# State@W in 64x32 array tiles, and x transposed by DMA, in a PE-bound attention and GLU kernel

## The chip, the core, the metric

The kernel runs on one core of a Trainium2 chip. The metric is device microseconds of one execution. PE is the matmul engine, DVE the vector engine, ACT the scalar engine, POOL is GpSimd, and SP is the engine that issues the DMAs. "Granted clock" is the share of full speed that PE was allowed. PSUM is where matmuls leave their results; ACT or DVE copies these out, which the text calls evacuation. A weight load (PEld) brings PE the stationary operand of a matmul. A profile is one execution; its span is 1.7 to 2.0 us shorter than that execution's time. Times between starts of instructions in a profile repeat to a few hundredths of a microsecond; whole executions of a kernel vary by 2 to 3 us.

## The reference

```python
# attention: B, H, S, Ns, D = 8, 8, 512, 32, 64
scores = x @ state^T / sqrt(D);  a = softmax(scores, -1);   xread = a @ state
scores2 = state @ x^T / sqrt(D); a2 = softmax(scores2, -1); sread = a2 @ x
y = concat([xread, sread], axis=2)            # per batch 512 + 32 rows of 512
# GLU: d_model 512, d_ff 1536
out = (sigmoid(y @ w_gate) * (y @ w_val)) @ w_out
```

Both kernels use that (a @ state) @ W = a @ (state @ W), so the 512 xread rows of a batch never exist; the product state@W (SW) does, once for each batch.

## The kernel before

A batch is worked on in twelve steps f. In step f PE computes a part of the output of batch b-1, then one block of gate and value (`gv`) of batch b, and between them pieces for batch b+1: one PSUM tile of SW, and at certain steps a piece of attention.

```python
p_gv  = tile_pool(bufs=3, PSUM); p_out = tile_pool(bufs=1, PSUM)
p_sw  = tile_pool(bufs=2, PSUM); p_at  = tile_pool(bufs=2, PSUM)

def at_xT(b, i):                 # x transposed on PE, copied out by DVE
    for jj in range(2):
        for c in range(4):
            nc.tensor.transpose(ps[:, jj, c], xbs[b][:, c, ...], ident)
    nc.vector.tensor_copy(xTs[b][:, 2*i:2*i+2], ps)

def sw_tile(b, t):               # one PSUM tile: heads of two j; half of each operand is zero
    for jj in range(2):
        lo = j * 128 - 64 * jj
        nc.tensor.matmul(ps, flat[:, lo:lo + 128], W[:, j, q*512:(q+1)*512], ...)
    nc.scalar.activation(SWs[b][:, g, w, q*512:(q+1)*512], ps, AF.Copy)

def gv(b, f):                    # two PSUM tiles, two matmuls each
    ...
    nc.scalar.activation(th, pss[0], AF.Tanh, scale=0.5)
    nc.vector.scalar_tensor_tensor(glus[b][:, f], th, 1.0, pss[1], ALU.add, ALU.mult)

    # one step, b > 0
    out_mm(b - 1, f); gv(b, f); sw_tile(nb, f)
    # f: 0, 1 at_xT   2, 3 at_S (scores, exp)   4, 5 at_norm   6 at_aT   8 at_sr
```

`at_norm` (DVE) makes `ab`, the normalised attention; `at_aT` transposes it on PE; `at_sr` is sread. Batch 0 runs while the weights are loaded and cast. "Batch 8" is no batch of its own: it is the GLU of the 256 sread rows of all batches.

The softmax here doesn't subtract the row's maximum and nothing guards it: scores larger than these inputs give would overflow.

## Time and profile before

| | before |
|---|---|
| time, median of 3 runs | 279.37 us (279.27 to 280.76) |
| span of the profiled run (another execution, of 281.71 us) | 279.9 us |
| first gv matmul | 20.62 us |
| batch 1 begins (first output matmul) | 54.02 us |
| one of batches 1 to 6 | 28.94 us (the sixth 28.74) |
| batch 7 begins | 227.44 us |

A batch's beginning is read from the order of time: the start of its first group of output matmuls. The difference between two beginnings is what a batch costs, waits included, and it is free of the overlap that makes a sum of durations misleading. The lines themselves stand in the prediction.

### The profile page before, as it was taken

The numbers are of one execution on the slowest core, as the hardware profiler recorded it, in microseconds if no ns is written. First come the engines' busy times: TensorE is split into PE (matmuls) and PEld (weight loads), VectorE is DVE, ScalarE is ACT, GpSimd is POOL, SyncE is SP. The second block draws the span as 40 slices with busy tenths as digits, with TensorE's granted clock in tenths as the row PEclk, the third lists the DMA queues.
The fourth block names the chain that finished last, engine by engine and source line by source line (L and its number), as shares of the span: only waits on it lengthen the run. The fifth ranks groups of instructions, "written<-read, shape, count | busy, mean of one in ns | idle before, by whom it ended". The sixth has DMA issues, their size and how long they took to land.

```text
span 279.9 us, 4309 instructions
## 1 busy us (share of the span) xinstructions
PE 260.1 (93%) x1670; PEld 136.5 (49%) x1670; DVE 132.0 (47%) x212; ACT 153.0 (55%) x264; POOL 40.4 (14%) x86
## 2 busy tenths in 40 slices
PE   6588857999999999999999999999999999999993
PEld 6564322554545454544554455445454544456651
DVE  4376273646544554446543744385338523332210
ACT  3368684656555755575557555655575554433220
POOL 1360089004000500050003100220010000000000
PEclk9979796999999999999999999999999999999999
DMA  7999738010016100611160015100101110110213
GB/s 239 368 378 386 250 115 290 3 41 37 37 32 174 42 27 31 187 40 37 39 190 37 37 41 176 51 37 37 40 37 39 40 39 37 75 40 37 77 39 75
DMA packets 18245, 27.55 MB, mean 98 GB/s; under 512 B 944, under 2 KB 9136, under 8 KB 18224
## 3 DMA queue, kind: packets, MB, share of 16 engines
q1 hardware_dynamic: 18224, 27.27, 28.8%
q8 instruction: 13, 0.21, 0.3%
q14 instruction: 8, 0.07, 0.1%
HBM read 18.35 MB, written 8.91 MB: 97 GB/s over the span
## 4 chain that ended last, share of the span: by engine, by line
PE 81%; DVE 10%; ACT 4%; issue 1%; DMA 1%; ACTq 0%
PE outp L209 29%; PE gvp L192 26%; PE swp L177 13%; PE gvp L195 4%; PE xTp L107 3%; DVE glu L200 2%; DVE rs L131 2%; DVE ab L134 2%; PE aTp L141 1%; DMA sf<-in_state_dram 1%; PE srp L157 1%; PE srp L152 1%; PE Sp L117 1%; DVE ri L133 1%; ACT th L199 1%
## 5 line engine op out<-in xcount | busy, mean ns | idle before, releaser
L200 DVE SCALAR_TENSOR_TENSOR glu<-th,gvp 128x512 bf16<-128x512 f32 (+1 forms) x108 | 70.9, 656 | 123.4 <-ACT th L199 108.0
L209 PE MATMUL outp<-wo,glu 128*128 128x512 bf16 x408 | 104.1, 379 | 0.7 <-ACT res L213 0.7
L192 PE MATMUL gvp<-aT,SW 128*128 128x512 bf16 x384 | 99.9, 382 | 0.1
L199 ACT ACTIVATE th<-gvp 128x512 f32<-128x512 f32 (+1 forms) x108 | 61.8, 572 | 63.4 <-PE gvp L192 53.0
L179 ACT ACTIVATE SW<-swp 128x512 bf16<-128x512 f32 x96 | 57.0, 597 | 29.1 <-PE swp L177 29.1
L192 PEld LDWEIGHTS <-SW 128*128 128x128 bf16 x384 | 37.6, 99 | 46.0 <-issue 1.6
L209 PEld LDWEIGHTS <-glu 128*128 128x128 bf16 x408 | 37.9, 98 | 37.9 <-issue 1.0
L177 PE MATMUL swp<-wg,sTz 128*128 128x512 bf16 x96 | 29.5, 396 | 7.1 <-DVE wg L92 7.1
L124 POOL CAST Eb<-E 128x256 bf16<-128x256 f32 x32 | 12.4, 416 | 160.4 <-ACT E L119 160.4
L177 PEld LDWEIGHTS <-sTz 128*128 128x128 bf16 x192 | 19.1, 101 | 31.4 <-DVE wg L92 7.7
L213 ACT ACTIVATE res<-outp 128x512 f32<-128x512 f32 x34 | 20.3, 597 | 21.0 <-PE outp L209 21.0
L177 PE MATMUL swp<-wv,sTz 128*128 128x512 bf16 x96 | 29.6, 398 | 0.3 <-ACT SW L179 0.3
L89 POOL CAST xb<-xf 128x512 bf16<-128x512 f32 x28 | 16.5, 628 | 0.0
L108 DVE COPY xT<-xTp 128x1024 bf16<-128x1024 bf16 x16 | 11.1, 691 | 4.1 <-PE xTp L107 4.1
L134 DVE TENSOR_TENSOR ab<-E,ri 128x512 bf16<-128x512 f32 x16 | 12.6, 788 | 0.6
L107 PE MATMUL xTp<-ident,xb 128*128 128x128 bf16 x128 | 10.4, 225 | 2.6 <-ACT xb L267 2.5
L107 PEld LDWEIGHTS <-xb 128*128 128x128 bf16 x128 | 8.8, 101 | 6.3 <-ACT xb L267 3.0
L131 DVE TENSOR_REDUCE rs<-E 128x16 f32<-128x512 f32 x16 | 10.8, 676 | 1.2 <-ACT E L119 1.2
L119 ACT ACTIVATE E<-Sp 128x512 f32<-128x512 f32 x16 | 9.4, 592 | 1.8 <-PE Sp L117 1.8
L160 DVE RECIPROCAL r<-srp 128x128 f32<-128x128 f32 x8 | 7.7, 957 | 3.1 <-PE srp L157 3.1
L97 POOL CAST wo<-wof 128x512 bf16<-128x512 f32 x12 | 8.7, 775 | 0.0
L227 PE MATMUL warm<-ident 128*128 128x128 bf16 x62 | 6.9, 301 | 1.4 <-POOL ident masks.py:199 1.4
(39 smaller groups left out, 111.1 us busy)
## 6 DMA issues: line engine op xcount, KB each, us to landing
out_dram<-res SPq DMA_DIRECT2D x32, 256.0 KB, 2.2
xf<-in_x_dram SPq DMA_DIRECT2D x7, 1024.0 KB, 6.4
wf<-in_moe_w_gate_dram SPq DMA_DIRECT2D x3, 1024.0 KB, 11.7
wf<-in_moe_w_val_dram SPq DMA_DIRECT2D x3, 1024.0 KB, 10.7
wof<-in_moe_w_out_dram SPq DMA_DIRECT2D x3, 1024.0 KB, 8.2
xf<-in_x_dram SPq DMA_DIRECT2D x2, 512.0 KB, 5.7
sf<-in_state_dram SPq DMA_DIRECT2D x1, 512.0 KB, 4.0
out_dram<-res SPq DMA_DIRECT2D x8, 64.0 KB, 1.7
```

The source lines that it names most:

```text
L89: eng.tensor_copy(xb.rearrange("p c h d -> p h c d")[:, 2 * i:2 * i + 2], xf[:, 2 * i:2 * i + 2])
L107: nc.tensor.transpose(ps[:, jj, c], xbs[b][:, c, 2 * j:2 * j + 2].rearrange("p h d -> p (h d)"), ident)
L124: nc.gpsimd.tensor_copy(Ebs[b][:, c], E1s[b][:, c])
L131: nc.vector.tensor_reduce(rs, E, AX.X, ALU.add)
L134: nc.vector.tensor_tensor(abs_[b][:, 2 * i:2 * i + 2].rearrange("p c (h n) -> p (c h) n", n=Ns), E, ri.unsqueeze(2).to_broadcast((128, 16, ...
L177: nc.tensor.matmul(ps, flat[:, lo:lo + 128], W[:, j, q * 512:(q + 1) * 512], start=(jj == 0), stop=(jj == 1))
L179: nc.scalar.activation(SWs[b][:, g, w, q * 512:(q + 1) * 512], ps, AF.Copy)
L192: nc.tensor.matmul(ps, SWs[b][:, g, w, fs], aTs[b][:, g], start=(g == 0), stop=(g == 1))
L199: nc.scalar.activation(th, pss[0], AF.Tanh, scale=0.5)
L200: nc.vector.scalar_tensor_tensor(glus[b][:, f], th, 1.0, pss[1], ALU.add, ALU.mult)
L209: nc.tensor.matmul(ops[b, c], glus[b][:, f, c * 128:(c + 1) * 128], wo[:, f], start=(f == 0), stop=(f == NF - 1))
L213: nc.scalar.activation(res, ops[b, c], AF.Copy, scale=0.5)
```

## The change

The intent: give PE less to do. The state operand of state@W was half zeros. The new kernel lets each 64x32 block (one head's 64 rows by 32 state columns) be a matmul of its own in its own part of the array: two row halves e times four column groups j, eight at a time. The eight go to two PSUM tiles; with gate and value a "visit" makes four, so the state@W pool takes four PSUM banks and the others give some up. x of batches 1 to 7 is transposed by DMA. The loads and casts of W come in column chunks.

```diff
-    p_gv  = ... bufs=3      p_sw = ... bufs=2      p_at = ... bufs=2
+    p_gv  = ... bufs=2      p_sw = ... bufs=4      p_at = ... bufs=1
-    stg = ... bufs=5
+    stg = ... bufs=6
+    def at_xT_dma(b):
+        for c in range(4):
+            nc.sync.dma_start_transpose(xT[:, :, c], xbs[b][:, c]...)
-    def sw_tile(b, t):  ...
+    def sw_visit(b, lo, n):
+        for w in range(2):
+            pss = [p_sw.tile((128, 512), FP)[:, :n] for e in range(2)]
+            for j in range(4):
+                for e in range(2):
+                    rows = slice(e * 64, (e + 1) * 64)
+                    nc.tensor.matmul(pss[e][j * Ns:(j + 1) * Ns], sTz[rows, b, j, e],
+                                     (wg, wv)[w][rows, j, lo:lo + n], start=True, stop=True)
+            for e in range(2):
+                sw_left.append((SWs[b][:, e, w, lo:lo + n], pss[e]))
     # one step, b > 0
-                sw_tile(nb, f)
+                if f % 4 == 0:
+                    sw_visit(nb, f * 128, 512)
+                sw_evac(act)                 # one of the four tiles a step
+                if f == 0:
+                    at_xT_dma(nb)
+                    if nb + 1 < B:
+                        load_x(nb + 1)
# cut: heads split by parity e in E1, Eb, ab; batch 0's schedule rewritten (visits at
# f = 1, 3, 3, 7, 7, 10, evacuated by ACT and DVE at once; casts of W at f = 3 and 7)
```

More of the change, by code (lines that the diff above doesn't have):

```diff
@@ L39 @@
     ctx.enter_context(tc.manual_schedule())
+    PS = bass.MemoryType.PSUM
     wp = ctx.enter_context(tc.tile_pool(name="wp", bufs=1))
-    stg = ctx.enter_context(tc.tile_pool(name="stg", bufs=5))
+    stg = ctx.enter_context(tc.tile_pool(name="stg", bufs=6))
     xp = ctx.enter_context(tc.tile_pool(name="xp", bufs=2))
@@ L45 @@
     fp = ctx.enter_context(tc.tile_pool(name="fp", bufs=3))
-    p_gv = ctx.enter_context(tc.tile_pool(name="p_gv", bufs=3, space=bass.MemoryType.PSUM))
-    p_out = ctx.enter_context(tc.tile_pool(name="p_out", bufs=1, space=bass.MemoryType.PSUM))
-    p_sw = ctx.enter_context(tc.tile_pool(name="p_sw", bufs=2, space=bass.MemoryType.PSUM))
-    p_at = ctx.enter_context(tc.tile_pool(name="p_at", bufs=2, space=bass.MemoryType.PSUM))
+    p_gv = ctx.enter_context(tc.tile_pool(name="p_gv", bufs=2, space=PS))
+    p_out = ctx.enter_context(tc.tile_pool(name="p_out", bufs=1, space=PS))
+    p_sw = ctx.enter_context(tc.tile_pool(name="p_sw", bufs=4, space=PS))
+    p_at = ctx.enter_context(tc.tile_pool(name="p_at", bufs=1, space=PS))
     ident = wp.tile((128, 128), BF, name="ident")
     ones = wp.tile((128, 2, 128), BF, name="ones")
-    sTz = wp.tile((128, B, 4, 128), BF, name="sTz")
+    sTz = wp.tile((128, B, 4, 2, Ns), BF, name="sTz")
     wg = wp.tile((128, 4, dff), BF, name="wg")
@@ L60, with psum_at, load_x, load_w @@
     E1s, Ebs, abs_, aTs, SWs, glus = {}, {}, {}, {}, {}, {}
-    def load_x(b):
+    vec, act, pool = nc.vector.tensor_copy, nc.scalar.copy, nc.gpsimd.tensor_copy
+    def psum_at(b):
+        return (p_sw, "swp") if b == 0 else (p_at, "at")
+    def load_x(b, parts=1):
         xf = stg.tile((128, H, 4, D), FP, name="xf", tag="stg")
         v = x[b].rearrange("h (p c) d -> p h c d", c=4)
-        if b == 0:
-            for i in range(2):
-                nc.sync.dma_start(xf[:, 4 * i:4 * i + 4], v[:, 4 * i:4 * i + 4])
-        else:
-            nc.sync.dma_start(xf, v)
+        n = H // parts
+        for i in range(parts):
+            nc.sync.dma_start(xf[:, n * i:n * i + n], v[:, n * i:n * i + n])
         xfs[b] = xf
-    def load_w(src, key, q):
-        wf = stg.tile((128, 4, 512), FP, name="wf", tag="stg")
-        nc.sync.dma_start(wf, src.rearrange("(k p) n -> p k n", p=128)[:, :, q * 512:(q + 1) * 512])
-        wfs[key, q] = wf
+    def load_w(src, key, lo, n):
+        wf = stg.tile((128, 4, n), FP, name="wf", tag="stg", padded_shape=(128, 4, 512))
+        nc.sync.dma_start(wf, src.rearrange("(k p) n -> p k n", p=128)[:, :, lo:lo + n])
+        wfs[key, lo] = wf
     def load_wo(q):
@@ L81, in load_wo, with cast_x, cast_w @@
         wfs["o", q] = wf
-    def cast_x(b, eng, parts):
+    def cast_x(b, cp, lo, n):
         if b not in xbs:
             xbs[b] = xp.tile((128, 4, H, D), BF, name="xb")
-        xf, xb = xfs[b], xbs[b]
-        for i in parts:
-            eng.tensor_copy(xb.rearrange("p c h d -> p h c d")[:, 2 * i:2 * i + 2], xf[:, 2 * i:2 * i + 2])
-    def cast_w(q):
-        nc.vector.tensor_copy(wg[:, :, q * 512:(q + 1) * 512], wfs["g", q])
-        nc.scalar.activation(wv[:, :, q * 512:(q + 1) * 512], wfs["v", q], AF.Copy)
+        cp(xbs[b].rearrange("p c h d -> p h c d")[:, lo:lo + n], xfs[b][:, lo:lo + n])
+    def cast_w(key, cp, lo, n, parts=1):
+        w, m = (wg if key == "g" else wv), 4 // parts
+        for i in range(parts):
+            cp(w[:, m * i:m * i + m, lo:lo + n], wfs[key, lo][:, m * i:m * i + m])
     def cast_wo(q):
@@ L97, in cast_wo, with xT_tile, at_xT_pe @@
             nc.gpsimd.tensor_copy(wo[:, 4 * q + i], wfs["o", q][:, i])
-    def at_xT(b, i):
-        if i == 0:
-            xTs[b] = ap_.tile((128, 4, 512), BF, name="xT")
-        ps = p_at.tile((128, 2, 4, 128), BF, name="xTp", tag="at")
+    def xT_tile(b):
+        if b not in xTs:
+            xTs[b] = ap_.tile((128, 4, 4, 128), BF, name="xT")
+        return xTs[b]
+    def at_xT_pe(b, i, cp):
+        pool_, tag = psum_at(b)
+        ps = pool_.tile((128, 2, 4, 128), BF, name="xTp", tag=tag)
         for jj in range(2):
@@ L107, in at_xT, with at_norm @@
                 nc.tensor.transpose(ps[:, jj, c], xbs[b][:, c, 2 * j:2 * j + 2].rearrange("p h d -> p (h d)"), ident)
-        nc.vector.tensor_copy(xTs[b][:, 2 * i:2 * i + 2], ps.rearrange("p j c t -> p j (c t)"))
+        cp(xT_tile(b)[:, 2 * i:2 * i + 2], ps)
+    def at_xT_dma(b):
+        xT = xT_tile(b)
+        for c in range(4):
+            nc.sync.dma_start_transpose(xT[:, :, c], xbs[b][:, c].rearrange("p h d -> p (h d)"))
     def at_S(b, i):
         if i == 0:
-            E1s[b] = ap_.tile((128, 4, H * Ns), FP, name="E1")
-        ps = p_at.tile((128, 2, H * Ns), FP, name="Sp", tag="at")
+            E1s[b] = ap_.tile((128, 4, 2, 4, Ns), FP, name="E1")
+        pool_, tag = psum_at(b)
+        ps = pool_.tile((128, 2, 2, 4, Ns), FP, name="Sp", tag=tag)
         for cc in range(2):
-            c = 2 * i + cc
             for j in range(4):
-                nc.tensor.matmul(ps[:, cc, j * 64:(j + 1) * 64], xTs[b][:, j, c * 128:(c + 1) * 128],
-                                 sTz[:, b, j, 0:64], start=True, stop=True)
+                nc.tensor.matmul(ps[:, cc, :, j], xTs[b][:, j, 2 * i + cc], sTz[:, b, j], start=True, stop=True)
         nc.scalar.activation(E1s[b][:, 2 * i:2 * i + 2], ps, AF.Exp, scale=scale)
     def at_Eb(b):
-        Ebs[b] = ap_.tile((128, 4, H * Ns), BF, name="Eb")
+        Ebs[b] = ap_.tile((128, 4, 2, 4, Ns), BF, name="Eb")
         for c in range(4):
             nc.gpsimd.tensor_copy(Ebs[b][:, c], E1s[b][:, c])
-    def at_norm(b, i):
+    def at_norm(b, i, eng):
         if i == 0:
-            abs_[b] = ap_.tile((128, 4, H * Ns), BF, name="ab")
-        E = E1s[b][:, 2 * i:2 * i + 2].rearrange("p c (h n) -> p (c h) n", n=Ns)
+            abs_[b] = ap_.tile((128, 4, 2, 128), BF, name="ab")
+        E = E1s[b][:, 2 * i:2 * i + 2].rearrange("p c e j n -> p (c e j) n")
         rs = ap_.tile((128, 16), FP, name="rs")
@@ L133, in at_norm @@
         nc.vector.reciprocal(ri, rs)
-        nc.vector.tensor_tensor(abs_[b][:, 2 * i:2 * i + 2].rearrange("p c (h n) -> p (c h) n", n=Ns), E,
-                                ri.unsqueeze(2).to_broadcast((128, 16, Ns)), ALU.mult)
+        eng.tensor_tensor(abs_[b][:, 2 * i:2 * i + 2].rearrange("p c e (j n) -> p (c e j) n", n=Ns), E,
+                          ri.unsqueeze(2).to_broadcast((128, 16, Ns)), ALU.mult)
     def at_aT(b):
-        ps = p_at.tile((128, 2, 4, 128), BF, name="aTp", tag="at")
-        for g in range(2):
+        pool_, tag = psum_at(b)
+        ps = pool_.tile((128, 2, 4, 128), BF, name="aTp", tag=tag)
+        for e in range(2):
             for c in range(4):
-                nc.tensor.transpose(ps[:, g, c], abs_[b][:, c, g * 128:(g + 1) * 128], ident)
+                nc.tensor.transpose(ps[:, e, c], abs_[b][:, c, e], ident)
         aTs[b] = ap_.tile((128, 2, 512), BF, name="aT")
@@ L147, in at_sr @@
         ps = p_at.tile((128, 512), FP, name="srp", tag="at")
-        sr = ps[:, 0:256].rearrange("p (j e) -> p j e", j=4)
+        sr = ps[:, 0:256].rearrange("p (j e n) -> p j e n", j=4, e=2)
         sm = ps[:, 256:384].rearrange("p (j n) -> p j n", j=4)
-        for par in range(2):
+        for e in range(2):
             for c in range(4):
-                nc.tensor.matmul(sm, ones[:, par],
-                                 Eb[:, c].rearrange("p (j e n) -> p j e n", j=4, e=2)[:, :, par],
-                                 start=(par == 0 and c == 0), stop=(par == 1 and c == 3))
+                nc.tensor.matmul(sm, ones[:, e], Eb[:, c, e], start=(e == 0 and c == 0), stop=(e == 1 and c == 3))
         for j in range(4):
@@ L157, in at_sr @@
                 nc.tensor.matmul(sr[:, j], xbs[b][:, c, 2 * j:2 * j + 2].rearrange("p h d -> p (h d)"),
-                                 Eb[:, c, j * 64:(j + 1) * 64], start=(c == 0), stop=(c == 3))
+                                 Eb[:, c, :, j], start=(c == 0), stop=(c == 3))
         r2 = ap_.tile((128, 4, Ns), FP, name="r2")
@@ L161, in at_sr, with sw_evac @@
         for e in range(2):
-            nc.vector.tensor_tensor(XS[e * 64:(e + 1) * 64, :, b * Ns:(b + 1) * Ns],
-                                    sr[e * 64:(e + 1) * 64, :, e * Ns:(e + 1) * Ns],
-                                    r2[e * 64:(e + 1) * 64], ALU.mult)
-    def sw_tile(b, t):
-        if t == 0:
-            SWs[b] = fp.tile((128, 2, 2, dff), BF, name="SW", bufs=2)
-        q, w, g = t // 4, (t // 2) % 2, t % 2
-        ps = p_sw.tile((128, 512), FP, name="swp")
-        W = wg if w == 0 else wv
-        for jj in range(2):
-            j = 2 * g + jj
-            flat = sTz[:, b].rearrange("p j e -> p (j e)")
-            lo = j * 128 - 64 * jj
-            nc.tensor.matmul(ps, flat[:, lo:lo + 128], W[:, j, q * 512:(q + 1) * 512],
-                             start=(jj == 0), stop=(jj == 1))
-        nc.scalar.activation(SWs[b][:, g, w, q * 512:(q + 1) * 512], ps, AF.Copy)
+            rows = slice(e * 64, (e + 1) * 64)
+            nc.vector.tensor_tensor(XS[rows, :, b * Ns:(b + 1) * Ns], sr[rows, :, e], r2[rows], ALU.mult)
+    sw_left = []
+    def sw_visit(b, lo, n):
+        if b not in SWs:
+            SWs[b] = fp.tile((128, 2, 2, dff), BF, name="SW", bufs=2)
+        for w in range(2):
+            pss = [p_sw.tile((128, 512), FP, name="swp", tag="swp")[:, :n] for e in range(2)]
+            for j in range(4):
+                for e in range(2):
+                    rows = slice(e * 64, (e + 1) * 64)
+                    nc.tensor.matmul(pss[e][j * Ns:(j + 1) * Ns], sTz[rows, b, j, e],
+                                     (wg, wv)[w][rows, j, lo:lo + n], start=True, stop=True)
+            for e in range(2):
+                sw_left.append((SWs[b][:, e, w, lo:lo + n], pss[e]))
+    def sw_evac(cp):
+        if sw_left:
+            cp(*sw_left.pop(0))
     def gv(b, f):
@@ L194, in gv @@
                 for j in range(4):
-                    nc.tensor.matmul(ps, (wg if w == 0 else wv)[:, j, fs], XS[:, j], start=(j == 0), stop=(j == 3))
+                    nc.tensor.matmul(ps, (wg, wv)[w][:, j, fs], XS[:, j], start=(j == 0), stop=(j == 3))
             pss.append(ps)
@@ L230 @@
     nc.sync.dma_start(sf, state.rearrange("b h (u l) d -> (b h u) l d", l=16))
-    load_x(0)
-    load_w(moe_w_gate, "g", 0)
-    load_w(moe_w_val, "v", 0)
+    load_x(0, 2)
+    load_w(moe_w_gate, "g", 0, 256)
+    load_w(moe_w_val, "v", 0, 256)
+    load_w(moe_w_gate, "g", 256, 256)
+    load_w(moe_w_val, "v", 256, 256)
     load_x(1)
@@ L236 @@
     nc.vector.memset(sTz, 0.0)
-    for par in range(2):
-        nc.gpsimd.memset(ones[:, par, par * 64:par * 64 + 64], 1.0)
-        nc.gpsimd.memset(ones[:, par, 64 - par * 64:128 - par * 64], 0.0)
+    for e in range(2):
+        nc.gpsimd.memset(ones[:, e, e * 64:e * 64 + 64], 1.0)
+        nc.gpsimd.memset(ones[:, e, 64 - e * 64:128 - e * 64], 0.0)
     pre = wp.tile((128, 1), FP, name="pre")
     nc.scalar.activation(pre, ident[:, 0:1], AF.Exp)
-    warm(30)
+    warm(36)
     sb = wp.tile((128, 16, 2, D), BF, name="sb")
     nc.vector.tensor_copy(sb[:, :, 0], sf)
-    nc.scalar.activation(sb[:, :, 1], sf, AF.Copy)
-    cast_x(0, nc.vector, (0, 1))
+    nc.scalar.copy(sb[:, :, 1], sf)
+    cast_x(0, vec, 0, 4)
+    cast_x(0, act, 4, 4)
     stp = []
@@ L255, with sT_copy @@
         stp.append(ps)
-    at_xT(0, 0)
-    for i in range(2):
+    def sT_copy(i, bs, cp):
         for e in range(2):
             rows = slice(e * 64, (e + 1) * 64)
-            dst = sTz[rows, :, :, e * Ns:(e + 1) * Ns].rearrange("p b j (u l) -> p (b j) u l", u=2)[:, :, :, 8 * i:8 * i + 8]
-            src = stp[i][rows].rearrange("p l (k e u) -> p k e u l", e=2, u=2)[:, :, e]
-            if e == 0:
-                nc.vector.tensor_copy(dst, src)
-            else:
-                nc.scalar.activation(dst, src, AF.Copy)
-    for i in (2, 3):
-        nc.scalar.activation(xbs[0].rearrange("p c h d -> p h c d")[:, 2 * i:2 * i + 2], xfs[0][:, 2 * i:2 * i + 2], AF.Copy)
+            dst = sTz[rows, bs, :, e].rearrange("p b j (u l) -> p (b j) u l", u=2)[:, :, :, 8 * i:8 * i + 8]
+            src = stp[i][rows].rearrange("p l (b j e u) -> p b j e u l", b=B, e=2, u=2)[:, bs, :, e]
+            cp(dst, src.rearrange("p b j u l -> p (b j) u l"))
+    at_xT_pe(0, 0, vec)
+    sT_copy(0, slice(0, 1), vec)
+    sT_copy(1, slice(0, 1), act)
+    cast_w("g", pool, 0, 256)
+    cast_w("v", pool, 0, 256)
     warm(8)
-    at_xT(0, 1)
-    load_w(moe_w_gate, "g", 1)
-    load_w(moe_w_val, "v", 1)
+    at_xT_pe(0, 1, vec)
+    load_w(moe_w_gate, "g", 512, 512)
+    load_w(moe_w_val, "v", 512, 512)
     warm(8)
@@ L274 @@
     at_S(0, 1)
-    for k in range(4):
-        nc.gpsimd.tensor_copy(wg[:, k, 0:512], wfs["g", 0][:, k])
-    at_norm(0, 0)
-    at_norm(0, 1)
-    nc.scalar.activation(wv[:, :, 0:512], wfs["v", 0], AF.Copy)
+    sT_copy(0, slice(1, B), act)
+    at_norm(0, 0, nc.vector)
+    at_norm(0, 1, nc.vector)
+    sT_copy(1, slice(1, B), act)
+    cast_w("g", pool, 256, 256)
+    cast_w("v", act, 256, 256)
     warm(16)
-    for t in range(2):
-        sw_tile(0, t)
+    sw_visit(0, 0, 256)
+    for cp in (act, act, act, act):
+        sw_evac(cp)
     at_aT(0)
     at_Eb(0)
-    at_sr(0)
-    cast_x(1, nc.gpsimd, range(4))
+    cast_x(1, pool, 0, 4)
+    cast_x(1, pool, 4, 4)
     for b in range(B + 1):
@@ L291 @@
             nb = b + 1 if b + 1 < B else None
-            if b == 0:
-                if f % 4 == 0:
-                    for t in range(f if f else 2, f + 4):
-                        sw_tile(0, t)
-                if f == 1:
-                    load_w(moe_w_gate, "g", 2)
-                    load_w(moe_w_val, "v", 2)
-                if f in (4, 5, 6):
-                    load_wo(f - 4)
-                if f in (8, 9, 10):
-                    cast_wo(f - 8)
             if b > 0:
@@ L305 @@
             gv(b, f)
-            if nb is not None:
-                sw_tile(nb, f)
-                if b > 0 and f == 0 and nb + 1 < B:
-                    load_x(nb + 1)
-                at = f if b > 0 else f - 2
-                if at == 0:
-                    at_xT(nb, 0)
-                elif at == 1:
-                    at_xT(nb, 1)
-                elif at == 2:
+            if b == 0:
+                if f == 1:
+                    sw_visit(0, 256, 256)
+                    for cp in (act, vec, act, vec):
+                        sw_evac(cp)
+                    load_w(moe_w_gate, "g", 1024, 512)
+                    load_w(moe_w_val, "v", 1024, 512)
+                    at_xT_dma(1)
+                elif f == 2:
+                    at_sr(0)
+                elif f == 3:
+                    sw_visit(1, 0, 512)
+                    for cp in (act, vec, act, vec):
+                        sw_evac(cp)
+                    cast_w("g", vec, 512, 512)
+                    cast_w("v", act, 512, 512)
+                    at_S(1, 0)
+                    sw_visit(0, 512, 512)
+                    for cp in (act, vec, act, vec):
+                        sw_evac(cp)
+                elif f == 4:
+                    at_S(1, 1)
+                    at_Eb(1)
+                elif f == 5:
+                    at_norm(1, 0, nc.vector)
+                elif f == 6:
+                    at_norm(1, 1, nc.vector)
+                elif f == 7:
+                    sw_visit(1, 512, 512)
+                    for cp in (act, vec, act, vec):
+                        sw_evac(cp)
+                    cast_w("g", vec, 1024, 512)
+                    cast_w("v", act, 1024, 512)
+                    at_aT(1)
+                    sw_visit(0, 1024, 512)
+                    for cp in (act, vec, act, vec):
+                        sw_evac(cp)
+                elif f == 9:
+                    at_sr(1)
+                elif f == 10:
+                    sw_visit(1, 1024, 512)
+                if f in (3, 5, 7):
+                    load_wo((f - 3) // 2)
+                if f == 8:
+                    load_x(2)
+                if f in (9, 10, 11):
+                    cast_wo(f - 9)
+                if f in (10, 11):
+                    sw_evac(act)
+                    sw_evac(vec)
+            elif nb is not None:
+                if f % 4 == 0:
+                    sw_visit(nb, f * 128, 512)
+                sw_evac(act)
+                if f == 0:
+                    at_xT_dma(nb)
+                    if nb + 1 < B:
+                        load_x(nb + 1)
+                elif f == 2:
@@ L316 @@
                     at_S(nb, 0)
-                elif at == 3:
+                elif f == 3:
                     at_S(nb, 1)
-                elif at == 4:
-                    at_norm(nb, 0)
+                elif f == 4:
+                    at_norm(nb, 0, nc.vector)
                     at_Eb(nb)
-                elif at == 5:
-                    at_norm(nb, 1)
-                elif at == 6:
+                elif f == 5:
+                    at_norm(nb, 1, nc.vector)
+                elif f == 6:
@@ L325 @@
                     at_aT(nb)
-                elif at == 8:
+                elif f == 8:
                     at_sr(nb)
-                if b == 0 and f == 9:
-                    load_x(2)
-                if nb + 1 < B and f == 11:
-                    cast_x(nb + 1, nc.gpsimd, range(4))
-            if b == 0 and f in (3, 7):
-                cast_w(f // 4 + 1)
+            if nb is not None and nb + 1 < B and f == 11:
+                cast_x(nb + 1, pool, 0, 4)
+                cast_x(nb + 1, pool, 4, 4)
```

## The prediction

> **What bounds the kernel now.** I read the page's busy table and slices first, then the costliest groups, then the order of time inside one batch, then the waits.
>
> ```profile
> PE 260.1 (93%) x1670; PEld 136.5 (49%) x1670; DVE 132.0 (47%) x212; ACT 153.0 (55%) x264; POOL 40.4 (14%) x86
> PE   6588857999999999999999999999999999999993
> PEclk9979796999999999999999999999999999999999
> L209 PE MATMUL outp<-wo,glu 128*128 128x512 bf16 x408 | 104.1, 379 | 0.7 <-ACT res L213 0.7
> L192 PE MATMUL gvp<-aT,SW 128*128 128x512 bf16 x384 | 99.9, 382 | 0.1
> L107 PE MATMUL xTp<-ident,xb 128*128 128x128 bf16 x128 | 10.4, 225 | 2.6 <-ACT xb L267 2.5
> ```
>
> PE is full from slice 7 on, at full clock; the two large groups wait for nothing. Before slice 7 it is not full. So there are two regimes: a start (batch 0, to 54.02 us, where the first output matmul begins) and a PE-bound rest. Mean durations overlap, so I use distances between starts. The order of time shows them (steps 5 and 6 of batch 3; columns: start, duration, group):
>
> ```profile
> 126.20 1.03 PE L209 MATMUL outp<-wo,glu 128*128 128x512 bf16 x4
> 127.04 0.67 DVE L131 TENSOR_REDUCE rs<-E 128x16 f32<-128x512 f32 x1
> 127.06 1.03 PE L192 MATMUL gvp<-aT,SW 128*128 128x512 bf16 x4
> 127.70 0.60 ACT L199 ACTIVATE th<-gvp 128x512 f32<-128x512 f32 x1 [0.70 <-PE gvp L192]
> 127.93 0.59 PE L177 MATMUL swp<-wv,sTz 128*128 128x512 bf16 x2
> 128.03 0.69 DVE L134 TENSOR_TENSOR ab<-E,ri 128x512 bf16<-128x512 f32 x1
> 128.36 0.93 PE L141 MATMUL aTp<-ident,ab 128*128 128x128 bf16 x8
> 128.64 0.68 DVE L200 SCALAR_TENSOR_TENSOR glu<-th,gvp 128x512 bf16<-128x512 f32 x1
> 129.12 1.03 PE L209 MATMUL outp<-wo,glu 128*128 128x512 bf16 x4
> ```
>
> Four matmuls of 512 columns take 127.06 - 126.20 = 0.86 us (0.216 each), two 0.43. Eight transposes take 0.44 in the order of time (142.99 to 143.43); here 128.36 to 129.12 = 0.76, because they wait 0.32 for `ab`. Eight 64-column matmuls take 0.23 (119.26 to 119.49), so 0.029 a pair of weight load and matmul. A batch repeats every 28.94 us (111.89 to 140.83): 120 x 0.216 = 25.9 for out, gv and state@W; x transposes 0.88; scores 0.46; a transposes 0.76; sread 0.91; sum 28.9. Six such batches, then batch 7 (20.86, no attention), batch 8 and the tail (31.8 from 248.16).
>
> ```profile
> DVE glu L200 <- ACT th L199: 108.0, 85, 4.9
> PEld L177 <- DVE wg L92: 7.7, 2, 5.6
> PE swp L177 <- DVE wg L92: 7.1, 2, 5.1
> ```
>
> The waits say that DVE's wait for tanh costs nothing now, and that in batch 0 PE lost 7.1 us to two waits for a cast of W. Outside these, PE has no wait of size.
>
> **What the Trainium skill says.** (1) "TensorE: Matmul & The Clock Gate", section Part 3 (packing small matmuls): 16 tiles of K=M=32, N=512 ran 10.6 times faster than one after another, a pack costing one matmul plus some 4 ns a tile. No run so far shows tiles here. (2) "TensorEngine Tiling (Array Packing)", section Tiling Modes, Key Properties: changing the tiling mode drains the engine; its PSUM Bottleneck section says evacuation gets no faster. The trace agrees on evacuation (0.60 us of ACT a tile, whatever wrote it) and shows no mode change. (3) "TensorE: Matmul & The Clock Gate", section Back-to-back issue gap: N/2.4 + 2.5 ns, 216 ns at 512; the trace has 0.216. (4) "VectorE: DVE Perf Modes", section The three transpose paths: a 128x128 bf16 transpose by DMA takes 1309 ns. The trace has no DMA transpose.
>
> **The change, part by part.** *State@W.* Before, 24 matmuls of 512 columns a batch, half of each stationary operand zeros: 24 x 0.216 = 5.2 us. After, three visits a batch, each 16 matmuls of 64x32 tiles (4 j, 2 row halves, g and v), eight at a time, giving the same 12 PSUM tiles. I estimate one visit as 16 pairs x 0.029 = 0.46, plus 0.19 for the last matmul to stream, 0.65 if nothing else; plus two mode changes, each estimated from the difference between a matmul's duration and its spacing, 0.379 - 0.216 = 0.16, and up to 0.1 of weight load that no longer hides. So V = 0.65 to 1.15; I choose 0.85. Three visits 2.55 in place of 5.2.
>
> *x transposes.* 16 PE transposes (0.88 us a batch) and two DVE copies (2 x 0.69) go. In their place four DMA transposes of 128x512 are issued by SP at step 0, first used at step 2.
>
> *PSUM.* gv goes from three buffers to two, attention from two to one, state@W from two to four. With two gv buffers the v half of step f+1 waits for the glu op of step f. With T the end of the g half: tanh starts T + 0.20 (126.20 to 127.70 with 1.29 of PE before it), ends T + 0.80, glu runs T + 0.84 to T + 1.53, PE may go on at T + 1.58. PE itself gets there at T + 0.43 + 0.86 + 0.43 = T + 1.72. It holds, with 0.14 us to spare. A result copy ahead of tanh (steps 2, 5, 8, 11) takes 0.17 of it: 0.03 lost there. The single output bank: copied out by 0.20 + 0.60 + 0.05 = 0.85 after its last matmul, wanted at 0.86. ACT has 18.0 us of work a batch (24 tiles and tanhs, 4 results, 2 exps at 0.60), so it isn't the bound.
>
> *The a transposes at step 6.* They wait for the second normalisation of step 5, which DVE starts after glu(5). A step without visit is 0.86 + 0.86 = 1.725 long now, 2.16 before. From the start s5 of step 5: result copy until 1.66, tanh 2.26, glu from 2.30, normalisation from 2.90 to 4.58 (1.68 as from 127.04 to 128.72). PE has done two transposes at s5 + 1.725 + 1.725 + 0.11 = 3.56 and waits until 4.63: 1.07, where it waited 0.32. So this block costs 1.07 + 0.44 = 1.5. Some 0.75 of the gain goes into a wait that was there before.
>
> *Sum for a batch:* 12 x 1.725 = 20.7; scores 0.46; sread 0.91; a transposes 1.5; visits 2.55; result copies 0.1: 26.2 in place of 28.9, 2.7 saved, six times 16.
>
> *Batch 0.* Gains: W in chunks of 256 lets the first gv start earlier (20.62 now; ACT's late x cast and the 1.9 us cast of wv go, I estimate 3 to 4 us), and six visits instead of 20 tiles save about 3.5 us of PE. Losses: gv follows its visit at once, so the evacuation (two of 0.6 on each of ACT and DVE, 1.4 with the wait) lies open three times, 4 us; two buffers without output matmuls between make a step 1.4 instead of 1.30; and batch 1's transposes stand in SP's queue behind the last two W loads, so the scores at step 3 can stall PE for some 5 us, in part instead of the 7.1 of waits now. I estimate 4 us saved, batch 1 beginning at about 50.
>
> *Batches 7, 8, tail:* unchanged, 0.2 lost to two buffers.
>
> Total: 279.4 - 16 - 4 + 0.2 = 259.6; I say 260.
>
> **Rivals.** *Transposes come late and become the bound.* PE reaches the scores at step 2, about 0.86 + 0.86 + 0.85 + 1.725 + 1.725 = 6.0 us after step 0 begins, the second half at 8.0. SP is nearly free (28.8% of DMA time in its queue), and x is cast at step 4 of the batch before, eight steps earlier (123.69 against 140.83), which speaks for being in time: at 1.3 us each one after another, the fourth lands near 6 to 7. Against: a transfer here is four 128x128 blocks; if each block took the skill's 1.3 us in turn, 21 us a batch, 15 over what is free, and the time would be near 350. A mild form (2 us each and 2 to land) stalls 1 to 2 us a batch: 266 to 272.
> *The tiles don't overlap.* A visit would be 16 x 0.216 = 3.5 us: 8 us a batch more than reckoned, 315 in all. For it speaks only that no trace here shows tiles.
> *Evacuation and buffers become the bound.* The margins of 0.14 and 0.01 us are thin. If tanh or a result copy queues behind a state@W copy (0.6), a step loses up to 0.5; at half the steps that is 3 us a batch, and the time 275 to 280: the gain moved into waits.
> *Better than reckoned:* V = 0.6 and no new wait at step 6 give 24.5 a batch, and a start 3 us better: 246 to 250.
>
> **Range and chances.** V alone moves the total by 6 us each way, the start by 4, small waits by 3 to 10 upwards. Hence 248 to 271. Slower needs one of the two hard failures, or waits that eat all; within 2% means above 273.8.
>
> **What would show it.** Right: batch starts 26 us apart; eight tile matmuls within some 0.3 us and a gap before and after them; PE waits of about 1 us for `ab` at step 6; no waits of scores for a DMA after batch 1; `gvp` matmuls waiting little for glu. Wrong: scores waiting for `xT` by DMA in each batch, gv matmuls waiting for DVE or ACT in most steps, visits over 1.3 us, or batch 1 beginning after 54.

## The result, and the profile after

The changed kernel takes 259.95 us (median of 4 runs, 259.11 to 260.76), the kernel before in the same rounds 280.06. The ratio is 0.9274, with a 95% interval of 0.9214 to 0.9334. A ratio is the mean time of one kernel's runs over that of the other's of the same rounds, so it isn't quite the ratio of the medians. The forecast was 260.

The page of the changed kernel, in the same rows as those shown of before (busy table, slices, and the costliest groups: busy time and mean duration in ns, then idle time before them and what ended it):

```profile
PE 230.8 (89%) x1772; PEld 112.4 (43%) x1772; DVE 127.8 (49%) x209; ACT 141.0 (54%) x259; POOL 40.1 (15%) x71
PE   6658483999899979998999799989998999999982
PEclk9968687799999999999999999999999999999998
L188 PE MATMUL swp<-wg,sTz 64*32 64x512 bf16 (+1 forms) x200 | 10.7, 400 | 2.7 <-DVE wg L97 2.7
L188 PE MATMUL swp<-wv,sTz 64*32 64x512 bf16 (+1 forms) x200 | 10.7, 394 | 1.5 <-ACT sTz L281 1.5
```

State@W is now made by 400 small matmuls that keep PE busy for 21.4 us, where 192 large ones took 59.1. PE is still the bound, but the row of its slices now has a hole in every batch (the 7s and lone 8s), and the start is emptier than before.

Who waited for whom on PE (total, times, longest, all in us):

```profile
PE aTp L154 <- DVE ab L146: 7.0, 7, 1.5
PE Sp L130 <- DMA xT<-xb: 3.9, 1, 3.9
PE swp L188 <- DVE wg L97: 2.7, 1, 2.7
```

The first is the hole in each batch: the transposes of the attention wait for the normalisation. The other two lie in batch 0. There is one wait for a DMA transpose and it is batch 1's; the later ones cost PE nothing.

Steps 4, 5 and 6 of batch 1, PE alone (start, duration, group):

```profile
61.13 1.03 PE L208 MATMUL gvp<-aT,SW 128*128 128x512 bf16 x4
62.08 0.41 PE L188 MATMUL swp<-wg,sTz 64*32 64x512 bf16 x8
62.31 0.40 PE L188 MATMUL swp<-wv,sTz 64*32 64x512 bf16 x8
62.64 1.04 PE L225 MATMUL outp<-wo,glu 128*128 128x512 bf16 x4
...
65.24 1.03 PE L208 MATMUL gvp<-aT,SW 128*128 128x512 bf16 x4
66.11 0.28 PE L154 MATMUL aTp<-ident,ab 128*128 128x128 bf16 x2
67.19 0.51 PE L154 MATMUL aTp<-ident,ab 128*128 128x128 bf16 x6 [0.81 <-DVE ab L146]
67.53 1.03 PE L225 MATMUL outp<-wo,glu 128*128 128x512 bf16 x4
```

The four gv matmuls end their streaming at 61.13 + 0.86 = 61.99. The first tile matmul starts 0.09 later; the next eight start 0.23 after the first eight; the output matmul starts 0.33 after those, 0.10 of it beyond a second group's 0.23. So a visit takes 0.65 us, of which 0.45 is matmuls and 0.2 is going in and out. Within a group the trace has the eight tile matmuls starting 0.003 us apart (62.084 to 62.107), so eight matmuls of 512 columns pass in little more than the time of one (0.23 and 0.216). Below, two transposes are done by 66.22 and the other six start at 67.19: 0.97 us between starts, of which the profile books 0.81 as idle.

Where the 20.9 us of span went:

| stretch | before | after | saved |
|---|---|---|---|
| up to batch 1 | 54.02 | 52.23 | 1.8 |
| batches 1 to 6 | 173.42 | 154.38 | 19.0 |
| batch 7 | 20.72 | 20.72 | 0.0 |
| batch 8 and tail | 31.8 | 31.7 | 0.1 |

The six batches take 25.51, 26.21, 25.51, 26.13, 25.50 and 25.52 us. An undisturbed batch saves 3.43 us: 3.2 by the visits (1.96 in place of 5.18), 0.88 by the x transposes, less 0.65 by which the wait for `ab` grew (0.97 in place of 0.32). The time was right to 0.1 us, but it was made of a start that saved 2 us less than forecast and batches that saved 3 us more. The experiments ask why.

### The profile page after: what moved, and what is told of

It reads as the page before. It is cut to its first block, busy times and chain, and to the rows that moved or that the text cites. A ratio compares the mean times of both kernels' runs of the same rounds, so it can differ in the third digit from the quotient of the medians.

```text
span 259.0 us, 4535 instructions
## 1 busy us (share of the span) xinstructions
PE 230.8 (89%) x1772; PEld 112.4 (43%) x1772; DVE 127.8 (49%) x209; ACT 141.0 (54%) x259; POOL 40.1 (15%) x71
## 4 chain that ended last, share of the span: by engine, by line
PE 75%; DMA 8%; DVE 8%; ACT 3%; SPq 2%; issue 2%; POOL 1%; ACTq 0%; DVEq 0%
PE outp L225 33%; PE gvp L208 28%; PE swp L188 4%; DMA xf<-in_x_dram 4%; PE gvp L211 4%; DMA xT<-xb 4%; DVE glu L216 2%; DVE ab L146 2%; ACT th L215 2%; PE Sp L130 2%; SPq L80 2%; PE srp L165 2%; DVE rs L143 1%; PE srp L168 1%; PE aTp L154 1%
## 5 line engine op out<-in xcount | busy, mean ns | idle before, releaser
L208 PE MATMUL gvp<-aT,SW 128*128 128x512 bf16 x384 | 104.0, 394 | 3.1 <-ACT SW L195 0.8
L195 ACT CAST SW<-swp 128x512 bf16<-128x512 f32 (+1 forms) x88 | 49.4, 571 | 7.9 <-PE swp L188 7.2
L92 POOL CAST xb<-xf 128x1024 bf16<-128x1024 f32 x14 | 14.5, 1061 | 12.4 <-PE gvp L208 7.5
L154 PE MATMUL aTp<-ident,ab 128*128 128x128 bf16 x64 | 6.5, 231 | 8.1 <-DVE ab L146 7.0
L188 PE MATMUL swp<-wg,sTz 64*32 64x512 bf16 (+1 forms) x200 | 10.7, 400 | 2.7 <-DVE wg L97 2.7
L188 PE MATMUL swp<-wv,sTz 64*32 64x512 bf16 (+1 forms) x200 | 10.7, 394 | 1.5 <-ACT sTz L281 1.5
L130 PE MATMUL Sp<-sTz,xT 128*128 128x64 bf16 x128 | 7.0, 199 | 4.2 <-DMA xT<-xb 3.9
L188 PEld LDWEIGHTS <-sTz 64*32 64x32 bf16 x400 | 3.8, 90 | 14.7 <-issue 10.7
L130 PEld LDWEIGHTS <-xT 128*128 128x128 bf16 x128 | 6.2, 102 | 8.4 <-DMA xT<-xb 4.6
L154 PEld LDWEIGHTS <-ab 128*128 128x128 bf16 x64 | 4.5, 102 | 11.3 <-DVE ab L146 8.2
```

Source lines behind the costliest of these rows:

```text
L92: cp(xbs[b].rearrange("p c h d -> p h c d")[:, lo:lo + n], xfs[b][:, lo:lo + n])
L130: nc.tensor.matmul(ps[:, cc, :, j], xTs[b][:, j, 2 * i + cc], sTz[:, b, j], start=True, stop=True)
L154: nc.tensor.transpose(ps[:, e, c], abs_[b][:, c, e], ident)
L188: nc.tensor.matmul(pss[e][j * Ns:(j + 1) * Ns], sTz[rows, b, j, e], (wg, wv)[w][rows, j, lo:lo + n], start=True, stop=True)
L195: cp(*sw_left.pop(0))
L208: nc.tensor.matmul(ps, SWs[b][:, g, w, fs], aTs[b][:, g], start=(g == 0), stop=(g == 1))
```

## The experiments

All ran with five rounds beside the kernel before; r1 to r4, r5 to r8, r9 and r10, and r11 and r12 each shared a chip. Each edit is against the changed kernel.

### r1_after: the changed kernel again

> The changed kernel again, as the base for the runs of this call. Every theory: 259 to 261 us, ratio to the kernel before near 0.927. In its profile PE waits for ab at step 6 of each of six batches, 0.8 us or 1.4 to 1.5 us.

Measured: 259.28 us, ratio 0.9261 (0.9220 to 0.9302). Batch 1 began at 51.09, and the batches took 25.51 (five times 25.51 or 25.52, once 25.62). So the base is confirmed; the long batches of 26.2 are not in every execution. 25.51 is the undisturbed batch.

### r5_full_rows: are eight tiles really concurrent?

```diff
-                    rows = slice(e * 64, (e + 1) * 64)
+                    rows = slice(0, 128)          # in sw_visit; the other half of sTz is zero
```

> The state@W matmuls read all 128 rows (the other half of the state tile is zero, so the result is the same): 128x32 tiles, four at a time, not eight 64x32. Theory (eight ran at once, 0.226 us a group in the trace): each group becomes two rounds, a visit grows by 2 x 0.216 = 0.43 us, an undisturbed batch goes from 25.51 to 26.8, six batches 7.8 us, batch 0 up to 2.6: 266 to 270 us. Rival (the two row halves did not run at once, and the gain is from the four column tiles): unchanged, 259 to 260.

Measured: 267.0 us, ratio 0.9505; an undisturbed batch takes 26.81. A visit of this run:

```profile
78.93 1.03 PE L208 MATMUL gvp<-aT,SW 128*128 128x512 bf16 x4
79.89 0.63 PE L188 MATMUL swp<-wg,sTz 128*32 128x512 bf16 x8
80.33 0.61 PE L188 MATMUL swp<-wv,sTz 128*32 128x512 bf16 x8
80.88 1.04 PE L225 MATMUL outp<-wo,glu 128*128 128x512 bf16 x4
```

The groups are now 0.44 apart in place of 0.23: two rounds of four. The rival is out: the row halves run at once, and that half of the concurrency is worth 1.3 us a batch. The four column groups were not taken apart by a run; that they too run at once is read from the starts.

### r6_split: what does a change of tiling mode cost?

```diff
-                if f % 4 == 0:
-                    sw_visit(nb, f * 128, 512)
+                if f % 2 == 0:                    # gate or value alone
+                    sw_visit(nb, f // 4 * 512, 512, ((f // 2) % 2,))
```

> Six visits of eight matmuls a batch in place of three of sixteen; same matmuls. It adds three mode changes in and out. Theory (from the trace, a visit of 0.66 us is 0.45 of matmuls and 0.2 of entering and leaving): 0.6 us a batch more, 26.1 where undisturbed, 3.6 us in all, 263 us. Rival (the change of mode costs nothing of its own, the gap is the weight load of the first tile): under 0.3 us a batch, 260.5.

Measured: 261.71 us, ratio 0.9303. A half visit of this run:

```profile
79.21 1.03 PE L208 MATMUL gvp<-aT,SW 128*128 128x512 bf16 x4
80.17 0.41 PE L188 MATMUL swp<-wg,sTz 64*32 64x512 bf16 x8
80.51 1.04 PE L225 MATMUL outp<-wo,glu 128*128 128x512 bf16 x4
```

From 80.07, where gv has streamed, to 80.51 is 0.44; two of them 0.88, against 0.65 for one whole visit. So going in and out costs 0.22, three times more a batch, as the theory said. But the undisturbed batch grew by 0.25 only (25.76), not by 0.66: the half visit at step 6 fills a part of the wait for `ab`. Four of the six batches took 25.95 to 26.05; in these the second normalisation's multiply took 0.89 to 0.90 in place of 0.69 us, which r8 explains. The time, 261.71, lies between theory (263) and rival (260.5); the cost per visit is the theory's. What it consists of stays open: each visit has both a change of mode and a first weight load that nothing hides, and r6 multiplies both.

### r4_pe_xT and r3_pe_x1: the transposes back on PE, all or batch 1's alone

```diff
# r3: in batch 0
-                    at_xT_dma(1)
+                    at_xT_pe(1, 0, vec)           # and at_xT_pe(1, 1, vec) at f == 2
# r4: also for nb > 1, at f == 0 and f == 1
-                    at_xT_dma(nb)
+                    at_xT_pe(nb, 0, vec)
```

> Batch 1's x is transposed on PE (steps 1 and 2 of batch 0), batches 2 to 7 by DMA as in the changed kernel. Theory: the 3.9 us wait of the scores for the transposes queued behind the W loads goes, 0.9 us of PE work comes, and wo and x loads no longer stand behind them: 256 to 257.5 us. Rival: the casts of W on DVE and ACT end only at 28.4 and 27.9 us, so the state@W visit that follows waits for them and little is gained: 259.

> All x transposes back on PE; state@W still as tiles. Theory (transposes by DMA cost PE nothing and save 0.88 us a batch): six batches 0.88 us longer each than in r3, 5.3 us, so 261.5 to 263 us if r3 gives 257. Rival (the DMA transposes disturb other transfers and the cast of x, and the two DVE copies are hidden): the difference to r3 is under 3 us, since the late x load of the changed kernel goes too.

Measured: r3 258.71 us (0.9216), r4 263.54 us (0.9413). In r4 each batch takes 26.40 or 26.41, 0.9 more than 25.51: what 16 transposes cost PE before. The difference r4 to r3 is 4.8 us, near the theory's 5.3 (r3 had two batches of 25.8 and 26.0). So the DMA transposes of batches 2 to 7 take this work off PE at no cost to it in these runs. The trace shows how much room they have: each of the four took 1.26 us to issue and 2.5 us from issue to landing (medians of 28).

```profile
xT<-xb SPq DMA_TRANSPOSE x28, 2.5
104.34 5.15 SPq L121 DMA_TRANSPOSE xT<-xb  x4
```

In batch 3 of the changed kernel SP issues them from 104.34 to 109.49, and PE needs the last for the scores of step 3, at 111.75, so about 1 us of room is left.

r3 shows the rival: the wait for the transposes went, and in its place the visit waits at the same point for the cast of W:

```profile
26.30 0.41 PE L130 MATMUL Sp<-sTz,xT 128*128 128x64 bf16 x8 [0.29 <-DVE XS L174]
29.35 0.63 PE L188 MATMUL swp<-wg,sTz 64*32 64x512 bf16 x8 [2.64 <-DVE wg L97]
```

The scores start 2.8 us earlier than in the changed kernel (29.09), the visit only 0.5 (29.85). The time is that of r1 within the noise; the forecast of 256 to 257.5 failed.

### r2_aT_step7: the wait at step 6, moved

```diff
-                elif f == 6:
+                elif f == 7:
                     at_aT(nb)
```

> The a transposes move from step 6 to step 7; nothing else. Theory A (the wait for ab is only a matter of where it stands): the six waits of 0.81, 1.5, 0.81, 1.35, 0.81, 0.81 us go, 6.1 us in all, time 253.5 to 254.5. Theory B (with two gv buffers part of the wait comes back): the v half of step 7 then waits for the glu op of step 6, which DVE runs after the normalisation; I reckon 0.4 us of such a wait in an undisturbed batch and 1.1 in a disturbed one, so only some 0.4 us a batch is gained, time 256.5 to 258, and new waits gvp <- glu show up.

Measured: 255.85 us, ratio 0.9124; an undisturbed batch takes 24.91, 0.60 less (one took 25.26). Step 7 of one batch:

```profile
115.28 1.03 PE L225 MATMUL outp<-wo,glu 128*128 128x512 bf16 x4
116.14 0.60 PE L208 MATMUL gvp<-aT,SW 128*128 128x512 bf16 x2
116.95 0.59 PE L208 MATMUL gvp<-aT,SW 128*128 128x512 bf16 x2 [0.22 <-DVE glu L216]
```

The gate half streams until 116.57 and the value half starts at 116.95: 0.38 us for a buffer that the glu op, delayed by the normalisation, still held. Theory B's mechanism and its 0.4 us are right; its time (256.5 to 258) was too high, because I had set the gain of removing the wait at 0.81 where between starts it is 0.97.

### r7_split_aT7_gv3: the third gv buffer

```diff
-    p_gv  bufs=2, p_sw bufs=4
+    p_gv  bufs=3, p_sw bufs=3        # with r6 and r2; batch 0's visits in halves too
```

> As r6, with the a transposes at step 7 and three gv buffers (state@W three). With two buffers the move gained 0.60 us in an undisturbed batch where the wait was 0.81. Theory (the missing 0.2 is the wait for glu that two buffers bring): here the move gains 0.8 a batch against r6, and no gvp <- glu wait is left from batch 1 on; about 5 us under r6, some 258. Rival (the 0.2 lies elsewhere): 0.6 a batch, 3.6 us under r6, 259.5.

Measured: 257.81 us, ratio 0.9177; every batch 25.22, no wait of gv for glu. The step from r6 is 0.54 to 0.83 a batch (r6 had 25.76 to 26.05). 24.53 (the sum of the matmuls, see r9) and three more mode changes of 0.22 make 25.19, so nothing else is waited for. The third buffer does remove the 0.38, but to get the bank for it the visits had to be split, which costs 0.66. Two buffers were the better use of PSUM.

### r8_x_early: the long batches

```diff
-                    if nb + 1 < B:                # at f == 0, after the four transposes
-                        load_x(nb + 1)
+                    if nb + 2 < B:                # at f == 8; x of batch 3 at the end of batch 0
+                        load_x(nb + 2)
```

> x of batches 3 to 7 is loaded at step 8 of the batch before last, not behind the four DMA transposes at step 0; nothing else. Theory (in the changed kernel the load comes so late that GpSimd's cast of x can fall on the second normalisation, whose multiply then takes 1.2 to 1.4 us in place of 0.69): all six batches take 25.51 us and all multiplies of steps 5 stay at 0.69; 0 to 1.4 us less than the changed kernel, 258 to 259. Rival (the slow multiply is not of the cast): long batches of 26.1 to 26.2 still show up.

In the changed kernel, the long batch that begins at 77.74 shows this on GpSimd and on DVE:

```profile
90.78 2.02 POOL L92 CAST xb<-xf 128x1024 bf16<-128x1024 f32 x2 [3.08 <-PE gvp L208]
91.95 1.39 DVE L146 TENSOR_TENSOR ab<-E,ri 128x512 bf16<-128x512 f32 x1
```

The multiply takes 1.39 us where it takes 0.69 alone, and PE then waits 1.50 in place of 0.81. The load of x stands in SP's queue behind four transposes of 5.15 us, so the cast runs after the load lands (at 90.58, just before the cast, though the view names a matmul as what it waited for), on top of step 5. Measured in r8: all twelve multiplies in batches 1 to 6 take 0.69 to 0.71, the casts begin at step 4, and the batches take 25.51 (one 25.59). The theory's mechanism holds. By itself this run could not show it, as r1 was nearly free of long batches too; the traces of all runs do. Wherever a cast of x began before a normalisation's multiply and ran over 0.15 us into it, the multiply took 0.69 us plus the overlap less 0.15: overlaps of 0.35, 0.46, 0.62, 0.69, 0.85 and 0.97 us (in r6, r3 twice, the changed kernel twice, and r11) made it 0.89, 1.00, 1.16, 1.23, 1.39 and 1.50. A cast that began after the multiply left it at 0.69. So the multiply got hardly anywhere until the cast was over. The theory's time doesn't show: 259.47 us, ratio 0.9227 (0.9198 to 0.9257), no different from r1, whose batches happened to be nearly all short.

### r9_norm_apart: no waits left?

```diff
-                elif f == 5:
+                elif f == 7:
                     at_norm(nb, 1, nc.vector)
-                elif f == 6:
+                elif f == 10:
                     at_aT(nb)                     # with r8's loads
```

> x loaded early as in r8; the second normalisation moves from step 5 to step 7 and the a transposes from step 6 to step 10, so that each normalisation's delay of glu falls into a step with a state@W visit, where PE has 0.65 us (step 4) or 1.6 us (step 8) more work. Theory: no wait for ab and none for glu is left in batches 1 to 6; a batch takes the sum of its matmuls, 24.53 us (25.51 less the wait of 0.97 between starts), 5.9 us in all: 253.5 us. Rival (some other buffer waits next: the single attention bank, the output bank): the batch stays at 24.9 as in r2, 256 us.

Measured: 253.3 us, ratio 0.9021 (0.8986 to 0.9056); all six batches take 24.53 us. Step 10 of one:

```profile
97.33 1.03 PE L208 MATMUL gvp<-aT,SW 128*128 128x512 bf16 x4
98.19 0.61 PE L154 MATMUL aTp<-ident,ab 128*128 128x128 bf16 x8
98.64 1.03 PE L225 MATMUL outp<-wo,glu 128*128 128x512 bf16 x4
```

The eight transposes run as one group in 0.45 us. 24.53 is the sum: twelve steps of 1.727 (20.73), three visits of 0.655 (1.96), scores 0.46, sread 0.92, transposes 0.45. So of the prediction's sum for an undisturbed batch, no term was off by over 0.1 us but the visits.

### r10_all: batch 0

```diff
# r9 and r3, and
-                    cast_w("g", vec, 512, 512)    # at f == 3; columns 1024 at f == 7
-                    cast_w("v", act, 512, 512)
+                    cast_w("g", pool, 512, 512, 2)   # all four at f == 2, on GpSimd
+                    cast_w("v", pool, 512, 512, 2)
```

> As r9, with batch 1's x transposed on PE as in r3 and the four casts of W's columns 512 to 1535 on GpSimd, which is idle from 20 to 30 us, not on DVE and ACT at steps 3 and 7. Theory (batch 0 has three waits in a row at step 3: the transposes, then the cast of W, and at step 7 the cast again, 2.7 us; r3 removed the first alone and gained next to nothing): both waits of 2.7 us go, batch 1 begins at 45 to 47 us, time 247 to 249. Rival (GpSimd's casts are slow beside a busy DVE, and its queue delays Eb and wo): batch 1 begins at 50 as in r3, 252 us.

Measured: 247.16 us (246.27 to 247.86), ratio 0.8807 (0.8772 to 0.8842); batch 1 begins at 44.82, and neither a wait of PE for the cast of W nor one for a DMA transpose is left. The theory holds: at step 3 the transposes and the casts were waited for side by side, so removing the transposes' wait alone (r3) gained nothing clear of the noise, and removing both does. No run moved the casts alone, so how the gain at step 3 divides is not shown; the 2.7 us at step 7 was the cast's alone. r10 is faster than both kernels.

### r11_fill and r12_all_fill: is it the low clock?

```diff
# r11, in batch 0
+    warm(20)
     at_aT(0)
+    warm(12)
...
+                    warm(40)                      # before at_S(1, 0)
+                    warm(28)                      # before sw_visit(0, 1024, 512)
# r12, on r10: warm(20) and warm(12) as above, and warm(12) after the
# evacuations of sw_visit(0, 512, 512) and of sw_visit(0, 1024, 512)
```

(`warm(n)` issues n matmuls of 128 columns on the identity, whose result nobody reads.)

> The changed kernel with PE's waits in batch 0 filled by matmuls of 128 columns on the identity (20 and 12 around the first a transposes, 40 before batch 1's scores, 28 before the state@W visit at step 7); no data changes. Theory (part of batch 0's time is the low clock that follows each wait: 0.50, 0.50 and 0.55 granted at 17.1 to 20.8, 29.1 to 33.3 and 43.2 to 49.2 us, which I reckon at some 5 us): the granted clock in these stretches rises, batch 1 begins 3 to 5 us earlier, 255 to 257 us. Rival (batch 0 is held by the loads, the casts and the evacuations; the slow matmuls are hidden behind them): within 1 us of the changed kernel, or slower by the filling.

> r10 with the same filling around the first a transposes, and 12 small matmuls each before the gv matmuls of steps 4 and 8, where PE waits for evacuations. There the low clock is left at 16.4 to 19.5 (0.60) and 37.8 to 41 us (0.52). Theory: 1.5 to 2.5 us less than r10, 245 us. Rival: unchanged, 247.

The suspicion came from the windows view of the changed kernel: after each wait of batch 0 PE ran at about half its clock (columns: stretch, length, busy time of PE, weight loads, DVE, ACT, GpSimd, then the granted clock, the DMA share and GB/s):

```profile
17.10:20.77 3.67, 3.66 (x10) 0.92 (x9) 0.69 (x1) 1.19 (x2) 2.02 (x2) 0.50 1.06 388
29.09:33.30 4.21, 3.89 (x36) 1.67 (x37) 1.41 (x3) 2.26 (x4) 0.74 (x2) 0.50 1.00 274
43.19:49.24 6.05, 5.77 (x48) 2.45 (x49) 3.20 (x5) 2.27 (x4) 2.94 (x4) 0.55 0.21 42
```

Measured: r11 258.88 us, ratio 0.9230 (0.9193 to 0.9266), not different from r1. The filling did what it should to the clock:

```profile
17.10:29.00 11.90, 7.57 (x108) 4.41 (x107) 7.29 (x12) 5.72 (x9) 2.02 (x2) 1.00 1.16 332
29.00:34.00 5.00, 3.96 (x38) 1.85 (x40) 1.98 (x3) 2.73 (x6) 0.74 (x2) 0.66 0.96 280
43.00:52.00 9.00, 7.34 (x78) 3.21 (x65) 7.01 (x12) 4.85 (x9) 2.72 (x4) 1.00 0.33 60
```

Yet the scores of batch 1 start at 29.19 (29.09 unfilled), because their transposes land no earlier. Batch 1 begins at 50.18, where the changed kernel's profiles have 51.09 and 52.23, and three longer batches (26.32, 25.58 and 25.74) gave back some 1 us. So my theory fell: at most 1 or 2 us of the start is the clock's, not 3 to 5. In r12 batch 1 begins at 43.50, 1.3 us before r10, but two batches took 25.04 and 25.43; in both, half of the scores waited for a DMA transpose (0.34 and 0.73 us booked). The time, 247.06, is that of r10, as the rival said and not the 245 of the theory. It is the thin room of the transposes, told at r4; what made them late in these two batches, I have not settled.

## Why the prediction was right

The time was forecast at 260 and is 259.95. That it agrees to 0.1 us is luck: two terms of the sum were off and made up for each other. The mechanism was right, and the signs that the prediction had named for it came: batch starts 25.5 to 26.2 us apart, eight tile matmuls within 0.03 us with a gap before and after, waits for `ab` of 0.97, no wait of the scores for a DMA after batch 1's. (One reading was off: batch 7 of the kernel before takes 20.72 us between starts, not 20.86.)

**The visit, V.** Forecast 0.85 us, measured 0.65. The forecast was 0.46 for 16 pairs of weight load and matmul one after another, 0.19 for the last one to stream, and some 0.2 for two changes of mode. The trace shows two groups, whose eight matmuls start together and stream together: 2 x 0.23 = 0.45, and 0.2 for going in and out (r6). So the 0.46 agrees by luck: it was reckoned at 0.029 us a pair, and the pairs follow at 0.003. The term that failed is the 0.19: the streaming is the 0.45 itself, and was counted twice. The 0.2 that was chosen for the changes of mode came true, though the upper estimates (0.16 to 0.26 each) were too high against 0.1 each. Three visits in six batches: 0.2 x 18 = 3.6 us better than forecast.

**The wait for `ab` at step 6.** Forecast 1.07, measured 0.97 between starts, when undisturbed, and 0.6 to 0.7 more in two of six batches, which I had not foreseen: the load of x behind the transposes, and the cast on the multiply (r8). That takes back 1.3 us. The claim that some of the gain moves into a wait that was there before is right; r9 shows that the wait is worth 0.98 us a batch.

**Two gv buffers.** Forecast to hold with 0.14 us to spare and to cost up to 0.1 a batch through result copies, 0.2 in batch 7. Measured: nothing. 24.53 in r9 is the bare sum, and batch 7 takes 20.72 as before. The margin is real, though: r2 used it up.

**The DMA transposes.** Forecast to be hidden, the fourth landing 6 to 7 us after the step's beginning. In batch 3 SP took up the first at 104.34, 0.4 us after the batch began, and the fourth three issues of 1.29 later, at about 108.2; with the median of 2.5 us to landing that is 110.7, 6.8 us after the beginning. The rival of late transposes is refuted for batches 2 to 7 in the changed kernel, though r12 met a mild form of it twice. The rival that the tiles don't overlap is refuted by the trace and r5.

**Batch 0.** Forecast 4 us saved; 1.8 in the profiled run, 2.9 in r1's. Right in it: the first gv matmul came at 17.10, 3.5 us earlier (3 to 4 forecast), and the scores waited 3.9 (some 5 forecast). The step that failed is "in part instead of the 7.1 of waits now". The items add up to the 4 us only with all 7.1 gone (3.5 + 3.5 + 7.1 - 4 - 1.2 - 5 = 3.9, where 1.2 is twelve steps of 0.1). So I counted the second wait for a cast of W as gone, and it is there: 2.7 us at step 7, since DVE starts its cast only after two evacuations, at 41.62, and ends it at 43.13. The changed kernel waits 3.9 + 2.7 = 6.6 us where the one before waited 7.1. r10 shows that taking away both waits for casts, with that for the transposes, is worth 6.5 us (51.30 in r9 to 44.82). The other items of batch 0 were not measured one by one. The low clock was no item of the forecast, and by r11 it is no large one.

Altogether: six batches saved 19.0 in place of 16, the start 1.8 in place of 4, and the end 0.1 in place of a loss of 0.2.

## What to carry to other kernels

When an operand is half zeros because its blocks are 64x32, array tiles made eight blocks pass in about the time of one here (0.23 us), so the fixed price of going in and out (0.2) is what to spread: few long visits, not many short ones. After such a cut, look at the helper engines' chains that had been hidden by the work removed, and place them in the steps that have the most PE work; here that was worth another 6 us at no cost. And where several waits end at about the same point, don't expect much from removing one: r3 took away a wait of 3.9 us, and the next visit started 0.5 us earlier.

## What the Trainium skill lacked or had wrong

- "TensorEngine Tiling (Array Packing)", section Tiling Modes, Key Properties, says that a change of mode drains the engine, with no figure. Here going in and out of 64x32 tiles, between full-array matmuls of 512 columns, took 0.20 to 0.22 us together, the first weight loads included (the changed kernel, r6).
- "VectorE: DVE Perf Modes", section The three transpose paths, has the DMA transpose for 128x128 only, 1309 ns. Here one of 128x512, four such blocks, took 1.26 us to issue and 2.5 us from issue to landing (medians of 28): less than twice the page's figure for one block, not four times. One block alone was not run.
